# RWKV-7 attention and a cosine feed-forward on one core: preparation, weights and first pieces placed in other chunks, with unread matmuls in the first waits

## The chip, the cores and the metric

The kernel runs on 1 core of a Trainium2 chip. The metric is the device time of one execution in microseconds (us), a median over executions.

## The reference

An RWKV-7 state recurrence per batch and head (4 batches, 8 heads, 768 steps, 40 columns), whose output, laid out as 3072 tokens by 320, goes through a feed-forward layer with a cosine:

```python
for t in range(S):
    y[:, :, t] = np.einsum('bhd,bhde->bhe', rt, state)
    Sa = np.einsum('bhde,bhe->bhd', state, at)
    state_decay = state * wt[:, :, None, :] - np.einsum('bhd,bhe->bhde', Sa, bt)
    state = state_decay + np.einsum('bhd,bhe->bhde', vt, kt)
...
h = x @ w_in                 # 320 -> 2048
g = h * np.cos(h)
return (g @ w_out).astype(np.float32)   # 2048 -> 320
```

The attention inputs are float32. The two weight matrices come as float64, so the kernel turns their words into float32 itself.

## The kernel before, in words

Time is cut into 24 chunks of 32 steps. All batches and heads of a chunk are handled together, as 128 partitions. The work has four kinds.

*Preparation* (`p1(c)`, lines 325 to 396) is made for two chunks at a time and needs nothing of the state. `p1_w` transposes `w` on TensorE and runs two products of decays as scans on VectorE (`wb`, line 335). `p1_a` transposes them back (`wn`), takes a reciprocal on VectorE (`rw`, line 356), multiplies `aT` (line 358), and has POOL make `bn` (line 361). `p1_b` transposes `bn`; `p1_n` multiplies `aT` and `bT` into `nps`, which ScalarE copies to `nt`.

*The inverse* of a triangular matrix is made for four chunks at once, on VectorE alone: `u` (line 401), 31 steps of two operations (`inv_tmp` line 409, `inv` line 413), and `rt` (line 417). `ch_s` of those four chunks reads `rt`.

*The chunk's own chain* is `p2_v`, `p2_k`, `p2_g` (letters v, k, g; made for the next chunk) and `ch_t`, `ch_q`, `ch_x`, `ch_s`, `ch_z` (t, q, x, s, z; with matmuls into `sT`, `qps`, `x0ps`, `sps`, `dps`). VectorE ends it with `qz` and `yt` (lines 597 and 604), then POOL and a round trip through DRAM make `xT`, the tokens.

*Pieces* are the feed-forward layer. One group of 256 tokens (two chunks) has four column blocks j. Each j has `first_a` and `first_b` (into `ph`, then turns, sine and product `gT` on ScalarE and VectorE) and, one j later, two `second` parts (into `po`). There are 192 pieces in a fixed list. `allowed(c)` lets a group's pieces begin at chunk 2g+2.

The *weights* are 20 blocks of 512 columns. Each block has four steps: `fetch` (a DMA on SP into one of a few slots), `taken` (VectorE lines 208 and 209, ScalarE 212 and 214), `mantissa` (VectorE 218, ScalarE 221) and `product` (VectorE 224, POOL 227). They stand in the list `w_steps`.

The order on every engine is the order in which the Python code issues work: no scheduler reorders it. In each chunk a list `segs` names the steps; `M` stands for one piece if any is allowed and due. `step` runs one step, then whatever `later` has put off by so many steps (loads, `kn`, tokens), then `fill[0]` steps of an inverse and `fill[1]` steps of the weights. Before a piece, weight steps are issued until its blocks are ready. Before `s`, pieces or inverse steps are issued until `rt` of the chunk is.

PSUM limits the order as well: `at` (preparation and chain) has two buffers of two banks each, `ph` has two buffers of one bank, `po` two. Before the change the lists of chunks 2 and 3 are:

```python
segs, fill = [t, v, pw, q, k, pa, x, g, M, pa1, s, M, z, M, M], (0, 3)      # chunk 2, p1(4)
segs = [t, M, pw, q, M, pa, pb4, x, M, pa1, pn4, M, pb, s, M, pn, M, z, M, v, M, k, g, M]   # chunk 3, p1(6)
```

Here `pw`, `pa`, `pa1`, `pb`, `pn` are the preparation's five steps, those with a 4 for chunks 4 and 5. The inverse of chunks 4 to 7 starts once `pn` of chunk 3 is issued.

Of the kernel before, what the change touches and what calls it, by code (L numbers as in the profile page):

```python
# [9 lines left out]
F32 = mybir.dt.float32  # L10
# [10 lines left out]
def kernel(  # L21
# [43 lines left out]
    nc = tc.nc  # L65
# [24 lines left out]
    def kept(name, shape, n=1, fill=None, part=lambda t: t, on=nc.gpsimd):  # L90

        tiles = []
        for i in range(n):
            t = const.tile(shape, F32, tag=f"{name}{i}", name=f"{name}{i}")
            if fill is not None:
                on.memset(part(t), fill)
            tiles.append(t)
        return tiles
# [47 lines left out]
    def load(c, names, via=nc.sync):  # L146
        for n in names:
            for i in range(B):
                via.dma_start(
                    nat[n, c][blk[i], :, :D],  # L150
                    src[n][i, :, c * C : (c + 1) * C, :].rearrange("h t d -> t h d"),
                )
# [16 lines left out]
    load(2, "a", nc.gpsimd)  # L169
    load(3, "a", nc.gpsimd)  # L170
    half_pi = kept("half_pi", [P, 1], 1, math.pi / 2)[0]
    rnd = kept("rnd", [P, 1], 1, ROUND)[0]
    w1 = kept("w1", [P, 4 * B, C], 2, 0.0, on=nc.vector)
    bn_b = kept("bn", [P, H, DP], 7, 0.0, padding, nc.vector)
# [3 lines left out]
    by_out = kept("by_out", [P, 1], 1, 2.0 * math.pi)[0]  # L178
    to_bits = kept("to_bits", [P, 1], 1, (127.0 - 1023) * 2**23)[0]

    zeros = const.tile([P, 4 * N72], mybir.dt.bfloat16, tag="zeros", name="zeros")
    nc.gpsimd.memset(zeros, 0.0)

    WID = 512
    first_done, second_done = [], []
# [120 lines left out]
    def later(steps, work):  # L306
        waiting.append([steps, work])
# [56 lines left out]
    def p1_b(c):  # L364
        ps = at("bT")
        for i in range(2):
            turned(ps[:, i], bn_b[(c + i) % 7])
        for i in range(2):
            bT = sb3.tile([P, 4, P], F32, tag="opT", name="bT")
            nc.scalar.copy(bT.rearrange("p j t -> p (j t)"), ps[:, i])  # L370
            G["bT", c + i] = bT
# [198 lines left out]
    def ch_z(c):  # L570
        ps = [at("dps") for _ in range(2)]
        sm = G["sm"]

        for bb in range(B):
            for e in range(2):
                mm(
                    ps[bb // 2][full[e], bb % 2, : 4 * N72], zeros[blk[bb], :DP],
                    zeros[blk[bb], : 4 * N72], True,
                )
        for s, n in ((0, kn_b[c % 2]), (1, bn_b[c % 7])):  # L580
            for j in range(4):
                o = C - C * (j // 2)
                for bb in range(B):
                    for e in range(2):
                        mm(
                            ps[bb // 2][half[e], bb % 2, j * N72 : (j + 1) * N72],
                            n[blk[bb], 2 * j + e, :D],
                            sm[e][blk[bb], j, :] if s else vvm[c % 2][blk[bb], 2 * j + e, o : o + N72],
                            False,
                        )  # L590
        wx, wc = G["wx", c], G["wc", c]
        yt = sb1.tile([P, 4, B, C], F32, tag="yt", name="yt")
        for bb in range(B):
            dp = ps[bb // 2][:, bb % 2]
            if c < NCH - 1:
                z = pick(qz[:, bb], C, (DP, 2), (NZ, 2), (1, D))
                nc.vector.tensor_tensor(z, pick(dp, 0, (2 * N72 + C, 2), (N72, 2), (1, D)), z, ALU.add)  # L597
                nc.gpsimd.tensor_tensor(  # L598
                    z, z,
                    wc.rearrange("p (f m b) -> p f m b", f=2, m=2)[:, :, :, bb]  # L600
                    .unsqueeze(3).to_broadcast([P, 2, 2, D]),
                    ALU.mult,
                )
            nc.vector.tensor_tensor(  # L604
                yt.rearrange("p (f m) b t -> p f m b t", f=2)[:, :, :, bb],
                pick(dp, D, (2 * N72 - D, 2), (N72, 2), (1, C)),
                pick(qz[:, bb], 0, (NZ - C, 2), (NZ, 2), (1, C)), ALU.add,
            )
        nc.gpsimd.tensor_tensor(  # L609
            yt.rearrange("p j b t -> p (j b) t"), yt.rearrange("p j b t -> p (j b) t"), wx, ALU.mult  # L610
        )
        later(2, lambda: tokens(c, yt))
# [114 lines left out]
    def p1(c):  # L727


        def last_a():  # L730
            p1_a(c + 1)
            if c >= 2 and c + 3 < NCH:
                for i in range(6):
                    later(9 + i // 3 if c == 2 else 2 + i, lambda i=i: load(c + 2 + i % 2, "wab"[i // 2]))

        return [lambda: p1_w(c), lambda: p1_a(c), last_a, lambda: p1_b(c), lambda: p1_n(c)]

    def p2(c):
        def last():
# [6 lines left out]
    def main(c):  # L746
        def last():
            ch_z(c)
            if c + 2 < NCH:
                later(1, lambda: p2_kn(c + 2))  # L750

        return [lambda: ch_t(c), lambda: ch_q(c), lambda: ch_x(c), lambda: ch_s(c), last]

    with tc.manual_schedule():
# [19 lines left out]
        def all_of(steps, n=None):  # L774
            for work in steps[:n]:
                work()
            del steps[:n]


        first, other = p1(0), p1(2)  # L780
        for seg in (*first[:3], *other[:3], *first[3:], *other[3:]):
# [15 lines left out]
                p2_kn(1)  # L797
        while inv_steps:
            inv_steps.pop(0)()
        for m in range(3, 5):  # L800
            w_work[m][0]()

# [7 lines left out]
            step(work, *fill)  # L810
            done += 1

        START = 2.4

        def allowed(c):
            return done < len(pieces) and 2 * pieces[done][0] + 2 <= c

# [1 line left out]
        for c in range(NCH):  # L819
            t, q, x, s, z = main(c)  # L820
            v, k, g = p2(c + 1) if c + 1 < NCH else [lambda: None] * 3
            q0 = c - c % 4 + 4
            fill, pn = (1, 4), None
            if c == 0:
                segs = [s, z]
            elif c == 1:
                segs = [t, v, q, k, x, g, s, z]
            elif c == 2:
                pw, pa, pa1, pb4, pn4 = p1(4)
                segs, fill = [t, v, pw, q, k, pa, x, g, M, pa1, s, M, z, M, M], (0, 3)  # L830
            elif c == 3:
                pw, pa, pa1, pb, pn = p1(6)
                segs = [
                    t, M, pw, q, M, pa, pb4, x, M, pa1, pn4, M, pb, s, M, pn, M, z, M, v, M, k, g,
                    M,
                ]
                fill = (2, 3)
            elif c == 4:
                pw, pa, pa1, *p8 = p1(8)
                segs = [t, M, v, q, M, k, x, M, g, M, s, M, z, M, pw, M, pa, pa1, M]  # L840
                fill = (3, 0)
            elif c == 5:
                pw, pa, pa1 = p1(10)[:3]
                pb, pn = p8
                segs = [t, M, pb, q, M, pn, v, M, x, k, M, s, pw, M, g, M, z, M, pa, pa1, M]
            elif c % 4 == 0 and q0 < NCH:
                pb, pn = p1(q0)[3:]
                segs = [t, v, M, q, M, k, x, M, g, M, s, pb, M, z, M, pn, M, M]
            elif c % 4 == 1 and q0 < NCH:
                pw, pa, pa1 = p1(q0 + 2)[:3]  # L850
                segs = [t, v, M, pw, q, M, k, x, M, g, M, s, M, z, M, pa, M, pa1, M]
            elif c % 4 == 2 and q0 < NCH:
                pb, pn = p1(q0 + 2)[3:]
                segs = [t, M, pb, q, M, pn, v, M, x, k, M, s, M, g, M, z, M, M]
            elif c % 4 == 3 and q0 + 4 < NCH:
                fill = (2 if c == 7 else 1, 0)
                pw, pa, pa1 = p1(q0 + 4)[:3]
                segs = [t, v, M, pw, q, M, k, x, M, g, M, s, M, z, M, pa, M, pa1, M]
            else:
                segs = [t, v, M, q, M, k, x, M, g, M, s, M, z, M, M, M]  # L860
            n = len(segs)

            goal = 8 * (c + 1) - (18 if c < 19 else 20)
            empty = segs.count(M) - (goal - done) if c > 6 else 0
            for i, seg in enumerate(segs):
                while seg is s and ("rt", c) not in G:
                    if allowed(c):
                        piece(4, 0)
                    else:
                        inv_steps.pop(0)()  # L870
                due = (c + (i + 1) / n - START) * 8
                while c == 3 and seg is pn4 and w_steps:
                    w_steps.pop(0)()
                if seg is not M:
                    step(seg, *fill, small=seg in (q, x, g, s, z, pn))
                elif empty > 0:
                    empty -= 1
                elif allowed(c) and (c > 6 or done < due + 1):
                    piece(*fill)
                while (M not in segs or i == n - 1) and done < (goal if c > 6 else due) and allowed(c):  # L880
                    piece(*fill)
                if seg is pn and (c == 3 or c > 4 and c % 4 == 2):
                    inv_steps.extend(inverse(q0))
# [36 lines left out]
```

## Time and profile before

| | |
|---|---|
| median of 8 runs | 855.88 us (854.88 to 859.67) |
| the profiled execution, its own time | 855.01 us |
| its span, first to last instruction | 853.2 us |
| TensorE matmul busy | 740.9 us (87%), 16664 matmuls |
| VectorE busy | 513.1 us (60%) |
| ScalarE busy | 376.1 us (44%) |
| POOL busy | 196.1 us (23%) |
| mean granted TensorE clock | 0.925 |

The profile calls TensorE PE, its weight load PEld, VectorE DVE, ScalarE ACT, GpSimd POOL and the DMA-issuing engine SP. Times are us unless marked ns. L101 is the line of the helper `mm` that records every matmul, so matmuls are told apart by the tile that they write. A float32 matmul of the program counts twice in the profile, so one j of a group has 24 matmuls into `ph` and 16 into `po`. The clock is a share of full speed.

### The profile page before, as it was taken

Reading aid. Unit: us, or ns where it says so; the run is one execution under the profiler, and the core shown is the slowest. Engines: PE = TensorE matmul, PEld = TensorE weight load, DVE = VectorE, ACT = ScalarE, POOL = GpSimd, SP = SyncE. Lnnn points to the kernel's source line nnn. Section 1 sums busy time; section 2 is a strip of 40 time slices with the busy share of each in tenths; the row PEclk is TensorE's granted clock in tenths of the full one; section 3 lists DMA queues with packets and bytes.
Section 4 is the critical chain, followed back from the end, with each engine's and each line's share of the span. In section 5 each row is a group of like instructions: output and inputs, shape, how many; then the busy total and the mean of one; then the engine's idle time right before and its main releaser. Section 6 shows DMA issues by size and latency. Waiting matters only on the chain.

```text
span 853.2 us, 37263 instructions
## 1 busy us (share of the span) xinstructions
PE 740.9 (87%) x16664; PEld 575.4 (67%) x16664; DVE 513.1 (60%) x1074; ACT 376.1 (44%) x706; POOL 196.1 (23%) x343
## 2 busy tenths in 40 slices
PE   3535445898899988999999999999999999999997
PEld 3424333676677766787777778777777777777775
DVE  8688687459756497335499435797245784323331
ACT  0216565344442532453553545435445453544343
POOL 4405543212113022122123203212121222101000
PEclk9755566798999998999999999999999999999999
DMA  7456353322031420421321312313302211101000
GB/s 99 100 88 192 98 150 96 65 42 42 26 70 39 67 56 21 72 58 26 64 62 41 75 36 54 62 36 66 75 17 43 44 40 46 27 20 35 19 16 15
DMA packets 181854, 49.08 MB, mean 58 GB/s; under 512 B 156992, under 2 KB 178496, under 8 KB 181696
## 3 DMA queue, kind: packets, MB, share of 16 engines
q1 hardware_dynamic: 179264, 46.05, 26.1%
q8 instruction: 131, 2.15, 1.0%
q10 hardware_dynamic: 2176, 0.33, 0.3%
q0 software_dynamic: 256, 0.33, 0.2%
q14 instruction: 27, 0.22, 0.1%
HBM read 38.80 MB, written 7.86 MB: 55 GB/s over the span
## 4 chain that ended last, share of the span: by engine, by line
PE 68%; DVE 19%; ACT 6%; issue 4%; DMA 2%; POOL 1%; SPq 0%; DVEq 0%; ACTq 0%
PE ph L101 24%; PE po L101 21%; DVE inv L413 4%; DVE inv_tmp L409 4%; PE dps L101 4%; PE x0ps L101 3%; PE gram L101 2%; PE sps L101 2%; DVE wb L335 2%; PE nps L101 2%; PE sT L499 2%; PE vT L293 2%; PE qps L101 1%; PE bT L293 1%; PE wn L348 1%
## 5 line engine op out<-in xcount | busy, mean ns | idle before, releaser
L101 PE MATMUL po<-w_out_sb,gT 128*128 128x320 f32 x768 | 229.9, 445 | 0.5 <-issue 0.5
L101 PE MATMUL ph<-xT,w_in_sb 128*128 128x256 f32 x768 | 190.8, 394 | 7.8 <-DVE gT L681 6.5
L101 PEld LDWEIGHTS po<-w_out_sb,gT 128*128 128x128 f32 x768 | 141.1, 192 | 55.8 <-issue 5.8
L101 PEld LDWEIGHTS ph<-xT,w_in_sb 128*128 128x128 f32 x768 | 142.9, 194 | 41.1 <-issue 19.6
L673 DVE SCALAR_TENSOR_TENSOR turns<-turns,ph 128x512 f32<-128x512 f32 x96 | 64.4, 684 | 126.5 <-ACT turns L671 126.3
L671 ACT ACTIVATE turns<-ph,rnd 128x512 f32<-128x512 f32 x96 | 64.7, 686 | 157.3 <-PE ph L101 156.9
L598 POOL TENSOR_TENSOR qz<-qz,wc 128x160 f32<-128x160 f32 x92 | 42.1, 475 | 261.0 <-DVE qz L597 260.4
L681 DVE TENSOR_TENSOR gT<-ph,turns 128x512 f32<-128x512 f32 x96 | 65.2, 686 | 37.9 <-ACT turns L678 37.8
L413 DVE TENSOR_TENSOR inv<-inv,inv_tmp 128x31 f32<-128x31 f32 (+15 forms) x186 | 69.9, 376 | 6.4
L409 DVE TENSOR_TENSOR inv_tmp<-u,inv 128x31 f32<-128x31 f32 (+15 forms) x186 | 70.6, 379 | 4.4
L678 ACT ACTIVATE turns<-turns,half_pi 128x512 f32<-128x512 f32 x96 | 69.3, 722 | 3.1
L677 ACT ACTIVATE turns<-turns 128x512 f32<-128x512 f32 x96 | 59.9, 624 | 17.5 <-DVE turns L673 17.5
L101 PE MATMUL ph<-xT,w_in_tail 64*128 64x256 f32 x384 | 55.5, 408 | 0.0
L356 DVE RECIPROCAL rw<-wn 128x320 f32<-128x320 f32 x24 | 51.6, 2150 | 2.4 <-PE wn L293 2.1
L503 ACT COPY s<-sT 128x512 f32<-128x512 f32 x46 | 24.5, 585 | 59.0 <-PE sT L499 59.0
L597 DVE TENSOR_TENSOR qz<-dps,qz 128x160 f32<-128x160 f32 x92 | 29.2, 318 | 27.3 <-PE dps L101 27.2
L487 ACT COPY vvm<-gram 128x256 f32<-128x256 f32 x24 | 8.9, 371 | 71.7 <-DVE ag L482 71.7
L101 PEld LDWEIGHTS ph<-xT,w_in_tail 64*128 64x128 f32 x384 | 33.6, 188 | 8.2 <-issue 3.8
L609 POOL TENSOR_TENSOR yt<-yt,wb 128x512 f32<-128x512 f32 x24 | 31.2, 1299 | 22.5 <-DVE yt L604 22.5
L101 PE MATMUL x0ps<-vvm,ag 32*32 32x72 f32 x1536 | 22.3, 239 | 13.8 <-ACT vvm L487 7.9
L431 POOL COPY vp<-nat_v 128x320 f32<-128x320 f32 x25 | 12.1, 484 | 94.2 <-DMA nat_v<-in_v_dram 54.5
L101 PE MATMUL sps<-x,rt 32*32 32x72 f32 x1536 | 22.6, 236 | 12.2 <-DVE rt L417 10.3
(111 smaller groups left out, 1048.5 us busy)
## 6 DMA issues: line engine op xcount, KB each, us to landing
words<-in_moe_w_in_dram SPq DMA_DIRECT2D x8, 512.0 KB
nat_k<-in_k_dram SPq DMA_DIRECT2D x96, 40.0 KB
nat_v<-in_v_dram SPq DMA_DIRECT2D x96, 40.0 KB
nat_r<-in_r_dram SPq DMA_DIRECT2D x96, 40.0 KB
xd<-yt SPq DMA_DIRECT2D x48, 80.0 KB
out_dram<-ot SPq DMA_DIRECT2D x24, 160.0 KB
nat_w<-in_w_dram SPq DMA_DIRECT2D x88, 40.0 KB
nat_b<-in_b_dram SPq DMA_DIRECT2D x88, 40.0 KB
```

Of the source, the lines that this page charges most:

```text
L101: nc.tensor.matmul(o, lhsT=lhsT, rhs=rhs, start=start, stop=stop, skip_group_check=True)
L356: nc.vector.reciprocal(rw, unpad(wn.rearrange("p (h d) -> p h d", h=H)))
L409: nc.vector.tensor_tensor(tmp, u[:, j : j + 1, :j].to_broadcast([P, C - j, j]), x[:, j:, j : j + 1].to_broadcast([P, C - j, j]), ALU.mult,)
L413: nc.vector.tensor_tensor(x[:, j:, :j], x[:, j:, :j], tmp, ALU.subtract)
L597: nc.vector.tensor_tensor(z, pick(dp, 0, (2 * N72 + C, 2), (N72, 2), (1, D)), z, ALU.add)
L598: nc.gpsimd.tensor_tensor(z, z, wc.rearrange("p (f m b) -> p f m b", f=2, m=2)[:, :, :, bb] .unsqueeze(3).to_broadcast([P, 2, 2, D]), ALU. ...
L609: nc.gpsimd.tensor_tensor(yt.rearrange("p j b t -> p (j b) t"), yt.rearrange("p j b t -> p (j b) t"), wx, ALU.mult)
L671: nc.scalar.activation(n, u, ACTF.Identity, bias=rnd, scale=1.0)
L673: nc.vector.scalar_tensor_tensor(n, n, -ROUND, u, ALU.add, ALU.subtract)
L677: nc.scalar.activation(n, n, ACTF.Abs)
L678: nc.scalar.activation(n, n, ACTF.Sin, bias=half_pi, scale=-2.0 * math.pi)
L681: nc.vector.tensor_tensor(gT[:, 2 * e : 2 * e + 2].rearrange("p f t -> p (f t)"), us[e], ns[e], ALU.mult)
```

## The change

It moves the preparation of chunks 4 and 5 from chunk 2 to chunk 3, where that of chunks 6 and 7 is too. Chunk 2 gets six places for pieces instead of four, all of them used (two first parts of j 0, two of j 1, two second parts of j 0). The weights are filled in at two steps per step in chunk 2 instead of three, so that blocks 16 to 19 fall into chunk 3. The loads of chunk 6 and 7's `w`, `a` and `b` now follow their readers in chunk 3 directly, and `kn` of chunk 4 is put off by eight steps.

From chunk 3 on, a chunk's places are either used or left empty by an even spread, instead of by a due time. That gives the same count of pieces by each chunk's end from chunk 4 on, but for one piece at chunk 19.

`busy` issues matmuls of zeros into a `ph` buffer that nobody reads: 58 behind the steps of chunks 0, 1 and the start of chunk 2, and two pairs in the tail of the first inverse, where a memset on VectorE releases them. A sine of one column is put at the kernel's start, so that the sine's table is loaded there.

```diff
+    warm = kept("warm", [P, 1])[0]
+    nc.scalar.activation(warm, half_pi, ACTF.Sin)
...
-    zeros = const.tile([P, 4 * N72], mybir.dt.bfloat16, tag="zeros", name="zeros")
-    nc.gpsimd.memset(zeros, 0.0)
+    idle = const.tile([P, 512], BF16, tag="idle", name="idle")
+    nc.gpsimd.memset(idle, 0.0)
+    tick = const.tile([P, 1], BF16, tag="tick", name="tick")
...
+        def first_w():
+            p1_w(c)
+            if c == 4:
+                for i in range(2):
+                    later(1, lambda i=i: load(6 + i, "w"))
+        def an_a(i):
+            p1_a(c + i)
+            if c == 4:
+                later(1, lambda: load(6 + i, "ab"))
...
-                later(1, lambda: p2_kn(c + 2))
+                later(8 if c == 2 else 1, lambda: p2_kn(c + 2))
...
+        def busy(n, after=False):
+            ps = ps_h.tile([P, 512], F32, tag="h", name="busy")
+            if after:
+                nc.vector.memset(tick, 1.0)
+                nc.tensor.matmul(
+                    ps[:1, :], lhsT=tick, rhs=idle, start=True, stop=True, skip_group_check=True
+                )
+            for _ in range(n):
+                mm(ps, idle[:, :P], idle, True)
...
         while inv_steps:
             inv_steps.pop(0)()
+            if 2 < len(inv_steps) < 9:
+                busy(1, True)
...
             elif c == 2:
-                pw, pa, pa1, pb4, pn4 = p1(4)
-                segs, fill = [t, v, pw, q, k, pa, x, g, M, pa1, s, M, z, M, M], (0, 3)
+                segs, fill = [t, v, q, k, M, x, M, g, M, s, M, z, M, M], (0, 2)
             elif c == 3:
+                pw4, pa4, pa5, pb4, pn4 = p1(4)
                 pw, pa, pa1, pb, pn = p1(6)
                 segs = [
-                    t, M, pw, q, M, pa, pb4, x, M, pa1, pn4, M, pb, s, M, pn, M, z, M, v, M, k, g,
-                    M,
+                    t, pw4, M, q, pa4, M, x, pa5, M, s, pw, M, pb4, pa, M, pn4, pa1, M, z, M, pb, v,
+                    pn, k, M, g,
                 ]
             elif c == 4:
-                segs = [t, M, v, q, M, k, x, M, g, M, s, M, z, M, pw, M, pa, pa1, M]
+                segs = [t, v, M, q, M, k, x, M, g, M, s, M, z, M, pw, M, pa, pa1, M]
...
-            empty = segs.count(M) - (goal - done) if c > 6 else 0
+            empty, places = 0, segs.count(M)
+            if c > 3:
+                empty = max(0, min(places - (goal - done), 2 if c < 8 else places))
+                goal = max(goal, done + places - empty)
...
+                    if c < 2 or c == 2 and not done:
+                        busy({s: 6, q: 5, v: 4, k: 4, z: 4}.get(seg, 3))
```

## The prediction

> **What bounds the kernel now.** I read the slices of the page first, then the sums by stage, then the chain that ended last, then the order in time of TensorE and VectorE around the stages that change.
>
> The slices show where TensorE is not the bound: about the first ten of the forty, where it has holes and a clock of half speed, while VectorE is full.
>
> ```profile
> PE   3535445898899988999999999999999999999997
> DVE  8688687459756497335499435797245784323331
> PEclk9755566798999998999999999999999999999999
> ```
>
> The sums by stage cut that start at events I found in the order in time: the first `sps` at 62.3, the end of chunk 1's `dps` at 101.9, the end of chunk 2's `qz` and `yt` at 152, VectorE's start on the second inverse at 188.3, its end at 224.1, the end of chunk 4's `dps` at 229.0. The first number is the length, then busy time per engine (x instructions), clock, DMA share, GB/s.
>
> ```profile
> 62.30:101.90 39.60, 19.76 (x740) 14.97 (x740) 29.08 (x55) 24.29 (x43) 19.03 (x18) 0.54 0.56 155
> 101.90:152.00 50.10, 24.63 (x588) 19.39 (x588) 41.39 (x72) 29.05 (x50) 23.48 (x28) 0.64 0.42 109
> 152.00:188.30 36.30, 34.06 (x646) 26.62 (x647) 15.19 (x22) 15.04 (x29) 7.08 (x14) 0.91 0.35 62
> 188.30:224.10 35.80, 29.75 (x691) 23.08 (x690) 32.77 (x82) 14.04 (x25) 5.95 (x11) 0.90 0.13 27
> 224.10:229.00 4.90, 4.90 (x212) 3.77 (x211) 2.22 (x7) 1.09 (x4) 0.00 (x0) 1.00 0.21 58
> 229.00:853.20 624.20, 603.35 (x13128) 466.66 (x13128) 342.86 (x733) 282.19 (x533) 120.92 (x222) 0.99 0.22 45
> ```
>
> VectorE carries the first two stages (29.1 of 39.6, 41.4 of 50.1), TensorE the third, VectorE again the fourth, TensorE all the rest. The two ends of the fourth stage, and the third stage's start, stand in the order in time (start, length, engine, line):
>
> ```profile
> 152.76 6.49 PE L101 MATMUL ph<-xT,w_in_sb 128*128 128x256 f32 x16 [6.46 <-DVE gT L681]
> ...
> 185.82 1.29 PE L101 MATMUL nps<-aT,bT 40*32 40x32 f32 x128
> ...
> 200.11 0.84 PE L101 MATMUL gram<-aT,kT 40*32 40x32 f32 x60 [3.02 <-ACT kT L462]
> ...
> 201.59 4.63 PE L101 MATMUL po<-w_out_sb,gT 128*128 128x320 f32 x8
> ...
> 224.57 0.88 PE L101 MATMUL sps<-x,rt 32*32 32x72 f32 x64
> ```
> ```profile
> 188.25 1.25 DVE L401 STREAM_TRANSPOSE u<-nt 128x1024 f32<-128x1024 f32 x1 [3.50 <-ACT nt L388]
> ...
> 222.23 1.97 DVE L417 STREAM_TRANSPOSE rt<-inv 128x1024 f32<-128x1024 f32 x1
> ```
>
> `nps` of chunks 6 and 7 ends at 187.1, ScalarE copies `nt`, VectorE starts `u` at 188.25, and 35.9 us later `rt` is there; `sps` of chunk 4 can't run before it, and does at once. So the time at which `u` starts sets the end of chunk 4, however much TensorE has done before.
>
> **The point of comparison.** In the built programs every engine's order is the same again from chunk 4's `dps` on (TensorE has then issued the same pieces: 64 `ph` and 32 `po` of the program in both), but for one piece that moves by one place in chunk 19, where TensorE is full. The 624 us behind it are a block that moves as a whole. So I forecast the shift of the `dps` end at 229.0. The profiled execution took 855.01 (span 853.2 and 1.8 around it), 0.87 below the median 855.88; the shift is taken from the median. 0.3% is 2.6 us, about what a measurement can tell from none.
>
> **To 62.3.** Two memsets of one column go into the inverse: 0.1 each by the nearest row (the `wT` memset, 0.09), +0.2. Four matmuls run in TensorE's wait of 10.3 for `rt`. The sine table's load moves from the chain to ScalarE's first idle stretch (6.4 us before 16.84), where it costs nothing:
>
> ```profile
> 146.95 1.28 ACT L678
> 148.24 0.72 ACT turns L678
> 148.96 0.62 ACT mant L221
> 149.61 0.69 DVE w_out_sb L224
> ```
>
> In the chain it stood in front of a weight block's last step and chunk 2's `qz`; -1.3 there, contained in the chain I build below.
>
> **Chunks 0 and 1 (62.3 to 101.9).** VectorE and ScalarE keep their order. TensorE gets 42 unread matmuls of 128x512 bf16. The trace has none; from below, the zeros (128x288 in four quarters) went by at eight in 0.33, so some 0.07 each for 512 columns; from above, a cold `ph` pass took 0.42 (3.39 for eight). I take 0.42 cold and 0.25 warm (1.99 for eight), the row that fills the array. Cold, groups of 3 to 6 take 1.3 to 2.5, and TensorE's waits here are 1.2 to 3.3; 20 us busy plus 16 make 36 of 39.6. So cold they just fit, and some links (`gram`, `dps`) come up to 1.5 later; warm, `dps` and `sps` come 1 to 1.5 earlier. I take 0, with both ends kept.
>
> Whether they warm the clock: the trace lost it in one idle of 3.0 (196.5 to 200.1: `po` then 4.63 against 2.32 elsewhere) and kept it in another of 3.0 (218 to 221). It came back only after 6.5 us of dense `ph` from 152.76. [...]
>
> **Chunk 2 (101.9 to 152).** It loses `wT`, two scans (2.34 and the memset 0.09), two reciprocals with their `aT` (2.75 each) and four of its eleven weight blocks (VectorE 0.42+0.42+0.69+0.69, 2.2 each): 16.7 of VectorE's 41.4. It gains one more first part: 2.6 on VectorE, 4.5 on TensorE. What is left is a chain through TensorE, which I lay from `qps`, still at 111.6 since it waits for `rT`: `qps` 1.3, five unread 2.1, `kT` 1.0, four unread 1.3 (half warm), first piece 2.6, `x0ps` 1.7, sixteen `ph` and tails 3.1: 124.7. Then the turn, sine and product of the first half: 3.6 in the clean instance after 160.3, and 1.7 for two weight steps queued between: `gT` at 130. The next piece needs that buffer of `ph` (rest before first): 3.4 cold, `sps` 1.2, `ph` 3.8 half warm, `dps` 1.7: 140.2. VectorE's turns and one weight block stand before `qz` and `yt` (1.8): 143.5, where before it was 152.0. The nine unread matmuls are 3.4 of this path; that is their price here, and what they buy is about 2 in warmer `ph` and `x0ps`.
>
> **Chunk 3.** What was taken out comes back. VectorE's list from 143.5 to `u`: four blocks with the slow forms that the trace shows beside POOL's sign product (1.38 for 0.42) and three pairs' leftovers, 14.4 with the scans of 4 and 5; four reciprocals with `aT` 11.0; the scans of 6 and 7, 2.45; turns and products of two groups 4.8; `x`, `sm`, `qz`, `yt` 2.7: 35.3 in all. TensorE's list is 43 at full clock from 140.2, so at least 183. Neither runs without waits: each reciprocal waits for its `wn`, and the next `wn` or `wT` for the `at` buffer which that chunk's `aT` frees. I take the 9 idle of VectorE in chunk 2's stage before, with the same alternation: `u` at 143.5 + 35.3 + 9 = 187.8. The bounds: 183 plus copies, 184; and with 15 of waits, 194.
>
> The DMAs move too: `words` of the last blocks wait on SP for their slots, chunk 6 and 7's `w`, `a`, `b` now queue behind chunk 4's and 5's readers, and `kn` of chunk 4 (POOL) waits 8 steps for its `rw`. By this schedule the last is issued near 166 and read at 176, so I cost it at nothing; if `nat_b` came late, `bT` and so `u` would slip by as much.
>
> **Chunk 4.** From `u` to `rt` before: 35.9. `qz`/`yt` (1.75), one pair of turns and products (2.6) and the steps slowed beside them (about 0.8) are now ahead of `u`; 0.3 is added: 31. So `rt` at 218.8 against 224.1, 5.3 earlier. But TensorE has only about 20 us of work between `nps` and this `sps` (32 before), so it stands idle for 9 or 10 and comes back cold: half of 5 us lost, as in the rows from 152.76 (6.49 for 3.98) and 201.59 (4.63 for 2.32): 2.4. Left: 2.9, and 855.9 - 2.9 = 853.0.
>
> **The rivals.** *More* (0.20): the unread matmuls keep the clock up through chunk 2 (`ph`, `sps`, `qps`, `kT` warm: 3.9 less) and `u` starts at 184: 855.9 - 6.8 = 849. For it: the occupancy of 36 in 39.6; against: the hole of 4 us before the second piece remains. *No net gain* (0.16): preparation is only moved, `u` at about 190.5, within 1.5 of before. *Slower* (0.24): preparation behind the last weights is a chain of PSUM turns, four reciprocals long, and it holds `nps` of chunks 6 and 7. It decides from `u` at 190.7 on (190.7 + 31 + 2.4 = 224.1); with 15 of waits, `u` at 194, the kernel takes 859. For it: VectorE's 35.3 in a stage where it had 15.2, and `nps` placed after chunk 3's `dps`; against: TensorE's order holds enough pieces between.
>
> **The numbers.** The forecast has 0.40: 851 to 855, two thirds of it below 853.3. Faster by over 0.3%: 0.26 + 0.20 = 0.46; within: 0.14 + 0.16 = 0.30; slower: 0.24. Most of *more* and *slower* is needed for 8 in 10: 847 to 860.
>
> **What would show it.** Right: `qz` of chunk 2 done near 143, `u` near 188, about 31 to `rt`, TensorE idle some 9 before that `sps` and cold after it, no table load after 20, the rest shifted as a block. Wrong: `u` before 185 or after 191; a clock near 1.0 from 62 to 140; chunk 1 ending over 2 us away from 101.9; or a new stall behind 229.

## The result and the profile after

The changed kernel takes **863.7 us** (median of 11, 860.6 to 868.2; a twelfth, at 872.4, is not in the median), 1.0079 times the time of the kernel before, 95% interval 1.0058 to 1.0101. It is 0.8% slower, and outside the range of the prediction. Its profiled execution took 860.64 us with a span of 858.6, against 855.01 and 853.2.

Slices of the page, after: TensorE is fuller in seven of the first ten slices and its clock higher in five, as if the change had done what it says.

```profile
PE   4547577995999979999989999989999989999997
DVE  8688868768555884345777255876354864323322
PEclk9659988996999989999999999999999999999999
```

Sums by stage, after, cut at its own events: first `sps`, end of chunk 1's `dps`, end of chunk 2's `qz` and `yt`, start of `u`, `sps` of chunk 4, end of chunk 4's `dps` (columns as before: length, busy time of PE, PEld, DVE, ACT, POOL, clock, DMA share, GB/s).

```profile
61.52:98.60 37.08, 24.55 (x772) 15.57 (x780) 29.08 (x55) 24.12 (x43) 18.66 (x18) 0.87 0.57 159
98.60:133.80 35.20, 28.43 (x618) 20.28 (x620) 26.87 (x55) 24.83 (x44) 15.79 (x18) 0.89 0.47 131
133.80:178.75 44.95, 37.71 (x812) 30.07 (x810) 33.25 (x50) 23.03 (x45) 20.71 (x34) 0.92 0.37 71
178.75:212.00 33.25, 21.78 (x516) 15.91 (x517) 28.59 (x73) 9.84 (x19) 1.34 (x2) 0.84 0.24 46
212.00:217.80 5.80, 5.80 (x210) 4.76 (x210) 0.52 (x3) 0.49 (x2) 0.00 (x0) 0.72 0.04 11
217.80:858.60 640.80, 610.20 (x13128) 470.51 (x13128) 343.60 (x733) 282.34 (x533) 120.71 (x222) 0.99 0.22 44
```

Chunk 4's `dps` ends at 217.8, 11.2 us *ahead* of 229.0. Then the last line, the "block that moves as a whole", takes 640.8 where it took 624.2: the same 13128 recorded matmuls at the same mean clock of 0.99, 16.6 us more. So the question is not why the early stages failed, since they gained more than I forecast, but what took back the gain in a stretch whose work the change hardly touches.

The order in time shows that the chain I followed is still there (VectorE's `u` and `rt`, TensorE's `sps` after it):

```profile
178.75 1.25 DVE L406 STREAM_TRANSPOSE u<-nt 128x1024 f32<-128x1024 f32 x1 [3.45 <-ACT nt L393]
...
209.94 1.91 DVE L422 STREAM_TRANSPOSE rt<-inv 128x1024 f32<-128x1024 f32 x1
```
```profile
212.00 1.25 PE L101 MATMUL sps<-x,rt 32*32 32x72 f32 x64 [7.35 <-DVE rt L422]
213.17 3.02 PE L101 MATMUL ph<-xT,w_in_sb 128*128 128x256 f32 x8
```

**Where the 16.6 us are.** The view of waits on TensorE behind 232 (us in total, times, longest) shows in the changed kernel what the kernel before does not have: TensorE stands still although nothing that the profile records is missing ("issue").

```profile
PE dps L101 <- issue: 7.5, 7, 1.9
...
PE ph L101 <- issue: 1.9, 2, 1.6
PE nps L101 <- issue: 1.6, 2, 0.8
PE x0ps L101 <- issue: 1.1, 1, 1.1
...
PE gram L101 <- issue: 0.2, 1, 0.2
```

These add up to 12.3. In the kernel before the same view has 0.7 of it:

```profile
PE po L101 <- issue: 0.5, 2, 0.3
...
PE kT L293 <- issue: 0.2, 1, 0.2
```

One of them, in the order in time of the changed kernel: 61 of the last 64 small `dps` matmuls run, then 1.92 of nothing, then the last two.

```profile
443.58 0.86 PE L101 MATMUL dps<-sm,bn 32*40 32x72 f32 x61
446.36 0.32 PE L101 MATMUL dps<-sm,bn 32*40 32x72 f32 x2 [1.92 <-issue]
```

The 61 of the same kind just before them had run, and the profile names nothing that the last two waited for. The same wait stands at 571.3 (1.93, before the last 12) and 692.0 (1.92, before the last 3): at nearly the same place of the program, every fourth chunk.

The first and the last of the three cost more than their wait. About 1 us behind each the granted clock falls to half for 3.4 us; the kernel before has full clock from 335.9 to its last 2 us (columns as in the sums by stage).

```profile
447.40:450.80 3.40, 3.40 (x11) 2.38 (x8) 1.68 (x5) 0.69 (x1) 3.33 (x5) 0.50 0.10 27
693.20:696.60 3.40, 3.40 (x10) 2.69 (x9) 3.06 (x5) 0.00 (x0) 3.39 (x4) 0.51 0.11 33
```

So the matmuls into `ph` behind the two waits take some 3.4 us longer: eight 3.42 instead of 1.99 and their tails 1.35 instead of 1.13, sixteen 5.41 instead of 3.62. That is part of why TensorE's busy time in the block, 610.20, is above the 603.35 of before.

The profile names no data that comes late in these waits, so I looked at the instructions. The page of the changed kernel has a queue by that name:

```profile
q8 instruction: 132, 2.16, 1.0%
```

132 packets of 2.16 MB are 16.4 KB each, and TensorE's 16717 matmuls and 16726 weight loads are 253 per packet. So a packet would be 256 instructions, 128 matmuls with their loads (the run f4 below shows it). In the first chunks of the kernel *before* the issue waits inside rows of small matmuls stand 127 or 128 recorded matmuls apart (87.40, 91.13, 100.78 us).

That gave **theory A**: the change adds 62 unread matmuls ahead of chunk 4 and nothing else that shifts TensorE's stream, so from there on every block boundary falls half a block elsewhere, on rows of small matmuls which use up a block faster than the next one comes. The rival theories are named with each experiment below.

### The profile page after: what moved, and what is told of

It is laid out like the page before. It is cut to its first block, busy times and chain, and to the rows that moved or that the text cites. A ratio compares the mean times of both kernels' runs of the same rounds, so it can differ in the third digit from the quotient of the medians.

```text
span 858.6 us, 37371 instructions
## 1 busy us (share of the span) xinstructions
PE 755.7 (88%) x16717; PEld 579.0 (67%) x16726; DVE 511.1 (60%) x1076; ACT 376.6 (44%) x707; POOL 196.8 (23%) x343
## 3 DMA queue, kind: packets, MB, share of 16 engines
q8 instruction: 132, 2.16, 1.0%
## 4 chain that ended last, share of the span: by engine, by line
PE 67%; DVE 20%; ACT 6%; issue 5%; DMA 1%; SPq 0%; ACTq 0%; DVEq 0%
PE ph L101 24%; PE po L101 19%; DVE inv_tmp L414 5%; DVE inv L418 5%; PE dps L101 4%; PE x0ps L101 3%; PE gram L101 2%; PE sps L101 2%; PE nps L101 2%; PE vT L298 2%; PE sT L504 2%; DVE wb L340 2%; PE qps L101 1%; PE wn L353 1%; DVE gT L686 1%
## 5 line engine op out<-in xcount | busy, mean ns | idle before, releaser
L101 PE MATMUL ph<-xT,w_in_sb 128*128 128x256 f32 x768 | 194.1, 399 | 3.8 <-DVE gT L686 3.7
L101 PEld LDWEIGHTS ph<-xT,w_in_sb 128*128 128x128 f32 x768 | 145.3, 197 | 37.5 <-issue 16.8
L508 ACT COPY s<-sT 128x512 f32<-128x512 f32 x46 | 24.5, 585 | 57.8 <-PE sT L504 57.8
L568 DVE TENSOR_TENSOR sm<-sps,su 128x128 f32<-128x128 f32 x48 | 11.7, 285 | 35.9 <-ACT sm L563 35.9
L101 PE MATMUL dps<-sm,bn 32*40 32x72 f32 x1536 | 25.3, 240 | 7.5 <-issue 7.5
```

What stands on the lines that cost most here:

```text
L101: nc.tensor.matmul(o, lhsT=lhsT, rhs=rhs, start=start, stop=stop, skip_group_check=True)
```

## The experiments

In the table "off" is how many matmuls the stream is off the kernel before's, modulo 128, behind the last insertion; "chunk 4" and "chunk 23" are how much earlier (-) or later the end of that chunk's `dps` is than in the kernel before (229.0, 795.7). These two are read from one execution of each kernel, the profiled one; those of g1 (867.2), f1 (853.0) and f3 (859.7) were the slowest of their runs, that of the changed kernel (860.6) its fastest.

| kernel | order | off | median us | ratio, 95% interval | chunk 4 | chunk 23 |
|---|---|---|---|---|---|---|
| the changed kernel | new | 62 | 863.7 | 1.0079 [1.0058, 1.0101] | -11.2 | +5.9 |
| e1_no_unread | new | 0 | 847.2 | 0.9855 [0.9819, 0.9891] | -9.2 | -9.3 |
| e2_after_whole_block | new | 0 | 844.1 | 0.9816 [0.9783, 0.985] | -8.6 | -10.9 |
| e3_before_half_block | old | 62 | 875.6 | 1.0181 [1.0147, 1.0215] | -0.5 | +21.5 |
| e4_before_whole_block | old | 0 | 855.8 | 0.9976 [0.995, 1.0001] | +2.4 | +1.6 |
| f1_pad98 | new | 32 | 850.5 | 0.9899 [0.984, 0.9957] | -12.0 | -3.2 |
| f2_pad34 | new | 96 | 857.9 | 1.0006 [0.9976, 1.0036] | | |
| f3_before_unread | old | 0 | 855.1 | 0.9986 [0.9957, 1.0014] | +1.5 | +4.6 |
| f4_dense_1024 | old | 0 | 879.5 | (one run) | +23.7 | +24.5 |
| g1_half_late | new | 0, from chunk 12 on 62 | 861.2 | 1.0044 [1.0019, 1.0068] | -8.6 | +12.5 |
| g2_after_mended_late | new | 62, from chunk 12 on 0 | 851.1 | 0.9925 [0.9898, 0.9951] | -10.1 | -3.8 |
| g3_whole_late | new | 0 | 848.1 | 0.9893 [0.9864, 0.9923] | -10.0 | -6.3 |

**Take the unread matmuls out** (e1_no_unread):

```diff
-            if 2 < len(inv_steps) < 9:
-                busy(1, True)
...
-                    if c < 2 or c == 2 and not done:
-                        busy({s: 6, q: 5, v: 4, k: 4, z: 4}.get(seg, 3))
```

> The kernel after without its 62 unread matmuls (124 fewer TensorE instructions); all else as after. Theory A (place of the instruction blocks: the late waits for nothing, 1.9 us each in dps, come because the 62 extra matmuls move TensorE's stream by half a block of 256 instructions): behind chunk 4 the waits are gone (under 1 us in all), the end of chunk 4 stays 6 to 11 us earlier than before, and the kernel takes 846 to 850 us. Theory B (the new order or the earlier start of the loads is what starves TensorE's fetching late, wherever the blocks lie): the late waits stay above 8 us and the kernel takes 858 us or more.

847.2 us: the loss behind chunk 4 is gone (-9.2 there, -9.3 at the end), and 1.1 us of issue waits are left behind 232, where under 1 was expected. But this takes away two things at once, the half block and whatever the unread matmuls do by themselves.

**Keep them and fill up the block** (e2_after_whole_block): 66 tiny matmuls ahead of the main loop, in TensorE's first wait for `rt`, which make 62 into 128.

```diff
+        pad = ps_h.tile([P, 512], F32, tag="h", name="pad")
+        for _ in range(66):
+            mm(pad[:C, :C], idle[:C, :C], idle[:C, :C], True)
```

> The kernel after with 66 more unread matmuls of 32x32, put where TensorE waits for the first rt, so that with the 62 they make 128 matmuls, one whole block of 256 instructions. Theory A: the late waits go as in the kernel before, though there are more unread matmuls than ever; lead of 11 us at chunk 4 kept to the end, 844 to 848 us. Theory B, and a theory C that more instructions as such cost time: late waits above 8 us, 860 us or more.

*More* unread matmuls, and 19 us less than the changed kernel: 844.1, the fastest of all kernels here. All that its waits behind 232 have left of "issue" is

```profile
PE sps L101 <- issue: 0.3, 1, 0.3
```

**Shift the old kernel** (e3_before_half_block with 62 tiny matmuls at that place, e4_before_whole_block with 128; nothing else changed):

```diff
+        pad = ps_h.tile([P, 512], F32, tag="h", name="pad")
+        for _ in range(62):   # 128 in e4
+            mm(pad[:C, :C], zeros[:C, :C], zeros[:C, :C], True)
```

> The kernel before, unchanged but for 62 unread 32x32 matmuls in TensorE's first wait for rt (some 2 us of work inside 10 us of waiting). Theory A: the order of pieces and preparation is innocent, so waits for nothing appear behind chunk 4 (10 us or more in all, 1.9 in dps of every fourth chunk) and the kernel takes 868 to 874 us. Theory B: no late waits, 855 to 858 us.

> The control: the kernel before with 128 unread 32x32 matmuls at the same place, a whole block. Theory A: no late waits, 855 to 858 us, although twice as much is added as in the run with 62. Theory C (added instructions cost): slower than the run with 62. Theory B: as before.

62 tiny matmuls in an idle stretch make the old kernel 1.8% slower, a little more than I had expected, and 128 leave it where it was. Chunk 4 still ends 0.5 early in e3; the 22 us come behind it, with the changed kernel's pattern:

```profile
PE dps L101 <- issue: 6.9, 7, 1.9
PE ph L101 <- issue: 2.5, 2, 1.4
PE nps L101 <- issue: 1.3, 2, 0.8
```

**Give the old order the unread matmuls and a whole block** (f3_before_unread: `busy`, which makes 74 matmuls here since in the old order the first piece comes later, and 54 tiny ones):

```diff
+            if 2 < len(inv_steps) < 9:
+                busy(1, True)
...
+        for _ in range(54):
+            mm(pad[:C, :C], idle[:C, :C], idle[:C, :C], True)
...
+                    if c < 2 or c == 2 and not done:
+                        busy({s: 6, q: 5, v: 4, k: 4, z: 4}.get(seg, 3))
```

> The kernel before with after's unread matmuls behind the same steps (74, since chunk 2 has more steps ahead of its first piece) and 54 of 32x32 in the first wait, one whole block in all; order of preparation, weights and pieces as before. If the warm clock is what made chunks 1 to 4 of after earlier, the end of chunk 4 comes 5 us or more earlier than before and the kernel takes 846 to 851 us; if the new order did, chunk 4 stays within 2 us, 854 to 858 us.

855.1: no gain, though the granted clock between 62 and 101 us rose from 0.54 to 0.76. With e1 (clock 0.54 there, chunk 4 9.2 ahead) that settles who earns the lead: the new order of preparation, weights and pieces does, the warm clock does not. (f3's end is 3.1 later than its chunk 4, with one late wait of 1.89 at 773.3.)

**Quarter blocks** (f1_pad98 and f2_pad34: e2 with 98 or 34 tiny matmuls instead of 66, so 32 or 96 off):

> The kernel after with 98 unread 32x32 matmuls in the first wait for rt (66 made a whole block with the 62; this is 32 matmuls, a quarter block, more). Theory A in its exact form: TensorE waits where a whole block of 256 instructions lies inside one run of small matmuls (dps, x0ps, nps, gram), since such a block is used up faster than the next one comes. Counting blocks of the built program from the place that the early waits show, this shift puts as many blocks behind chunk 4 into such runs as the kernel after has (some 10, against 2 with 66), so it is as slow as after: 857 to 864 us. Theory D, that loss grows with the distance from a whole block: a quarter block costs about half, 851 to 854 us.

> The kernel after with 34 unread 32x32 matmuls at the same place, a quarter block less than a whole one. Theory A in its exact form: only 2 or 3 blocks behind chunk 4 lie in a run of small matmuls, so 843 to 848 us, as with 66. Theory D: 851 to 854 us, as with 98, since both are a quarter block away.

Both missed the finer rule by which I had tried to say, block by block, which place costs how much: it wanted f1 slow and f2 fast, and it is the other way round. The profiled execution of f2 took 869.9, far above its median, so only its times are used. In f1 the issue waits behind 232 add up to 6.1, half of the changed kernel's 12.3. What stands is a hump: in the new order 844.1 at a whole block, 850.5 at 32, 863.7 at 62, 857.9 at 96. Why 96 costs more than 32 stays open.

**A long row of tiny matmuls** (f4_dense_1024: e3 with 1024 instead of 62, eight whole blocks):

> The kernel before with 1024 unread 32x32 matmuls in a row, eight whole blocks, in the first wait for rt: the rate of fetching by itself. Theory A: the first two or three blocks run at TensorE's own rate (1.3 to 1.7 us for 128 matmuls), then each block waits for the next, some 3 to 4 us for 128 (as a dps block of 1.5 us waited 1.9), 25 to 30 us for all; and behind chunk 4 no waits, since whole blocks were added. If fetching is no bound, all 1024 go in 14 us or less without a wait.

The row in the order in time:

```profile
54.87 10.48 PE L101 MATMUL pad<-zeros 32*32 32x32 bf16 x384 [1.02 <-issue]
65.50 3.57 PE L101 MATMUL pad<-zeros 32*32 32x32 bf16 x128 [0.16 <-issue]
70.33 10.48 PE L101 MATMUL pad<-zeros 32*32 32x32 bf16 x384 [1.25 <-issue]
```

384, 128 and 384 matmuls are multiples of the block, and the issue waits stand between them and nowhere else. The whole row took 31 us, 3.87 per 128, a little over the 25 to 30 expected, but not for the reason expected: 128 of these matmuls run for 3.5 themselves (10.48 for 384), where I had 1.3 to 1.7, and the waits are only 0.16 to 1.25 each. So this bounds the time that a block needs to come, but doesn't measure it. Behind chunk 4 little is lost (+23.7 there, +22.0 at chunk 18, +24.5 at the end, with one late wait of 1.88 at 794.9), nearly as whole blocks should have it.

**Late shifts.** All of these stand before chunk 4, so a rival was left: that the early stages set up something (buffers, DMAs, the order of loads) which costs later. So the shift was put at the start of chunk 12, where TensorE is full: 62 tiny matmuls into e2 (g1_half_late), 66 into the changed kernel (g2_after_mended_late), 128 into e2 (g3_whole_late).

```diff
+            if c == 12:
+                late = ps_h.tile([P, 512], F32, tag="h", name="late")
+                for _ in range(62):   # 66 in g2, 128 in g3
+                    mm(late[:C, :C], idle[:C, :C], idle[:C, :C], True)
             t, q, x, s, z = main(c)
```

> The version that is the changed kernel plus 66 tiny matmuls (844.1 us), with a further 62 tiny unread matmuls in a row at the start of chunk 12, where TensorE is full. Theory A (the place of 128-matmul blocks in TensorE's stream decides): until chunk 11 as in that version (dps ends some 8.5 us ahead of the kernel before), then, half a block off, what the changed kernel lost from chunk 11 to 23 (13.1 us), and 2 to 4 for the tiny matmuls themselves: 858 to 862 us, with late issue waits behind chunk 12 that recur every fourth chunk. Theory E (the loss is decided early, by how the warm stages, the DMAs and the buffers stand to each other): only the 2 to 4 us of the tiny matmuls, 846 to 848.

> The changed kernel with 66 tiny unread matmuls at the start of chunk 12, which with its 62 extra matmuls make a whole block from there on. Theory A: as the changed kernel until chunk 11 (dps end 7 us ahead of the kernel before), and from there no further loss: 863.7 less 13.1, and 2 to 4 for the tiny matmuls, 852 to 855 us, with the issue waits of 1.9 gone behind chunk 12. Theory E: 865 to 868.

> The version of 844.1 us with a further 128 tiny unread matmuls in a row (one whole block) at the start of chunk 12: the price of such matmuls where TensorE is full, without a change of phase. Theories A and E alike: 3.5 to 5 us (128 matmuls took 3.87 us in the run of 1024), 847.5 to 849; if it lost more than 8, added matmuls behind chunk 4 would cost by themselves and the two other late runs could not be read as a matter of place.

Half a block from chunk 12 on loses 20.9 us between chunks 11 and 23 (-8.4 to +12.5), where e2 gains 2.1 and the tiny matmuls themselves took 1.71. Mended from chunk 12 on, the changed kernel loses 2.7 there (-6.5 to -3.8, of which 1.81 are the tiny matmuls), instead of 13.1. (g1's profiled execution was 6 us above its median; by the medians half a block late costs 861.2 - 844.1 = 17.1.) A whole block costs 4.0 us in the time, 3.40 of it for its matmuls. g2 came 0.9 below its range and the other two within theirs; the theory by which the loss is settled early wanted 846 to 848 and 865 to 868 for the first two, and is out. TensorE's waits behind 462, in g1:

```profile
PE dps L101 <- issue: 8.1, 6, 1.9
PE nps L101 <- issue: 1.6, 2, 1.0
...
PE ph L101 <- issue: 1.1, 1, 1.1
```

and in g2, where the changed kernel still has 4.6 of `dps` behind 462 and this run none:

```profile
PE sps L101 <- issue: 0.8, 1, 0.8
```

**The packets in time.** The traces also hold each packet of that queue with its time. The 1024 matmuls of f4, with their loads 2048 instructions, bring 8 packets more than the kernel before has, so a packet is 256 instructions (the kernel before, then f4):

```profile
q8 instruction: 131, 2.15, 1.0%
q8 instruction: 139, 2.28, 1.0%
```

In the changed kernel a packet is under way from 444.02 to 445.09, and the wait of 1.92 ends at 446.36, 1.27 after it landed. All 13 issue waits of the changed kernel behind 232 end 1.27 to 1.54 after a packet has landed, though its packets are 6.5 us apart on average (858.6 / 132). The least that lies between the starts of two packets is 3.22 us in the changed kernel and 3.32 in the kernel before. Counted 128 matmuls back, the block that ran out there began at some 442.9 and was used up by 444.4, in 1.5 us; the next could begin only at 446.36. By these times what came late was the next block of instructions.

## Why the prediction was wrong

**The step that failed is the point of comparison:** "The 624 us behind it are a block that moves as a whole." It rested on the order of instructions being the same there, and it is; but 62 unread matmuls ahead of it moved every block boundary in it, and that cost 17.1 us from chunk 4 to 23. I priced the unread matmuls where they run (3.4 us in chunk 2) and never asked what they do to the place of all that follows. With the boundaries a whole block away, the early lead carries through: e2 is 8.6 ahead at chunk 4 and 10.9 at chunk 23, and takes 844.1. (The changed kernel's own lead alone would give 855.9 - 11.2 = 844.7; that the two agree so well is luck, since e2's lead is smaller and grows.)

The clue stood in the trace of before. Its waits on TensorE between 62 and 152 us hold lines that I had seen only as holes in a stage which VectorE bounds:

```profile
PE dps L101 <- issue: 4.1, 3, 2.1
...
PE gram L101 <- issue: 2.3, 2, 1.2
...
PE sps L101 <- issue: 1.4, 1, 1.4
```

For a wait in the midst of one row of equal matmuls the profile names no data that is late: the one of 2.14 at 100.78 ended 1.38 after a packet of instructions had landed. (Not every "issue" ends so soon behind a packet: `kT` has a wait of 3.3 in the same view, at 79.94, whose last packet had landed 3.9 before.) Behind 232 the same view had 0.7 of it in all, which says that this kernel's boundaries happened to lie well, and so that moving them could hardly gain and could well lose.

**The early part by its steps.** I forecast chunk 4's `dps` 2.9 earlier, and it was 11.2: 8.3 too little, made of these.

- *To 62.3:* +0.2 forecast, `sps` at 61.52, 0.8 earlier. The table load went to 10.63 in ScalarE's idle stretch and cost nothing: right.
- *Chunks 0 and 1, taken at 0:* 3.2 earlier. (Of my sum, 42 matmuls at 0.42 are 17.6 and not 16; it changes nothing here.) In before, 2.14 of issue stood ahead of the last 47 `dps` at 100.78; in the changed kernel none does. That too is place: e2, with the same unread matmuls and 66 more, has 3.36 there and ends chunk 1 0.1 late.
- *"`qps` 1.3, ... still at 111.6 since it waits for `rT`":* 105.50. Beyond chunk 1's 3.2 this is 2.9. In the changed kernel `qps` runs before ScalarE's copy `rT` (107.72) has begun, so it never needed that result: in before it had waited for the copy to free one of the two `at` buffers, since the `wT` of chunk 4 (108.72) held the other. I had counted the VectorE work that leaves with `wT`, but not its buffer.
- *`qps` to `gT`, 18.4 by my sum:* 15.6. The unread groups took what I gave them warm (four in 1.03, 0.26 each), but the first piece and its `x0ps` ran at full clock (1.89 for eight `ph`; I had 2.6). The next piece, after a hole of 3.75, was cold (3.75 for eight), as forecast.
- *`gT` to the end of `qz` and `yt`:* 13.5 forecast, 12.7 measured. The sum of these steps: 133.8 against 143.5.
- *Chunk 3, the longest sum:* 35.3 of VectorE's list and 9 of waits, 44.3; measured 45.0. That is luck in part: VectorE was busy for 33.25 of it and waited for 11.7, so two misses of 2 to 3 us cancel. So `u` at 178.75 is 9.05 earlier than forecast, all of it from chunk 1 and chunk 2.
- *Chunk 4:* `u` to `sps` 31 forecast, 33.25 measured; TensorE idle 9 to 10 forecast, 7.35 measured; from there to the `dps` end 7.3 forecast with the cold loss, 5.8 measured (`ph` 3.02 for eight, half cold).

**The clock.** I leant to cold groups (2.1 for the five behind `qps`; they took 1.25). That was my estimate, from the idles and the return of the clock in the kernel before, and the measurement is against it: the granted clock from 61.5 to 98.6 was 0.87, with TensorE busy 24.55 of 37.08 in pieces, where it was 0.54 in the kernel before and 0.54 in e1, which has no such groups. So short groups with holes of up to 3.36 between them did raise it here. Nor did the two idles of the kernel before give a rule: both were 3.02 long, and the clock fell in one of them (0.56 from 200.1 to 207.0) and not in the other (1.00 from 218 to 226). And it mattered little: e1, at 0.54 in that stage, is 9.2 ahead at chunk 4, and e2, at 0.81, 8.6.

**The rivals.** *Slower* named the nearest time (859) with the wrong mechanism: it needed `u` at 194, and `u` came at 178.75. *More* had the direction of the early part, but put it down to the clock, which, as e1 and f3 show, did not earn it. Of the four signs that I listed as showing it wrong, three came (`u` before 185, chunk 1's end 3.2 away, a new stall behind 229), and the last of these was the one that decided.

**What stays open.** Of the 17.1 us lost behind chunk 4, the waits show 12.3, less 0.7 before, and the two stretches at half clock some 3.4; the last 2 were not found line by line. Why a packet starts when it does is not shown. A whole block does not put everything back either: f3 and f4 each have one wait of 1.9 in chunk 23 that the kernel before has not. And the cost as a function of the shift is known at four places only (0, 32, 62 and 96).

## What to carry to other kernels

Before you call a stretch unchanged because its instructions are, count how many instructions the edit adds or removes ahead of it on the same engine, and look for "issue" waits inside rows of equal, ready instructions in the trace: where they end just after a packet of the instruction queue has landed (1.27 to 1.54 us after it here), the place of the stream's blocks is likely to be a cost (17.1 us here). Where a kernel has dense rows of small matmuls, test an edit with the stream filled up to a whole block (here 128 matmuls with their loads) as well, or a good change is read as a bad one: this one is 0.8% slower as written and 1.8% faster with 66 more matmuls that do nothing. The cheaper place for the fill was a wait that ends later anyway: 128 tiny matmuls there left the time where it was (e4, 0.9976), and at chunk 12, where TensorE is full, they cost 4.0 us (g3).

## What was new of the hardware

- TensorE's instructions came in units of 256 (132 packets of 16.4 KB for 33443 instructions of the changed kernel; 2048 instructions more brought 8 packets more in f4, 139 for 131). Inside dense rows of small matmuls single waits for which the profile names no late data reached 1.93 us behind chunk 4 of the changed kernel, and 3.36 in chunk 1 of e2. All 13 issue waits behind 232 in the changed kernel end 1.27 to 1.54 us after a packet has landed, and its packets start at least 3.22 us apart.
- Two of the changed kernel's three longest late waits (1.92 each) were followed by 3.4 us at half clock, which cost some 3.4 us more on the matmuls behind them.
- The same work is up to 2.3% apart by that place (844.1 and 863.7 in the new order, the faster with 66 tiny matmuls more), and in the changed kernel the longest waits recur every fourth chunk (446.36, 571.3 and 692.0).
- A row of 1024 matmuls of 32x32 had its waits 384, 128 and 384 matmuls apart, all multiples of 128 (f4); 128 of them ran in 3.40 us (g3) and 3.57 (f4) in a row.
- Groups of 3 to 6 unread 128x512 bf16 matmuls, with holes of up to 3.4 us between other work, held the granted clock at 0.87 from 61.5 to 98.6, where it was 0.54 in the kernel before and in e1. In that stage VectorE is busy 29.08 of 37.08, and they brought no time: f3, with the clock up from 0.54 to 0.76, took 855.1.
